# Kv and q loads gated by a step, four buffers for partial sums at a switch of segments, and one kv split moved

## The chip, the cores and the metric

The kernel runs on one core of one Trainium2 chip. Its time is the device time of one execution in microseconds (us), the median of several. TensorE (PE) multiplies, VectorE (DVE) and ScalarE (ACT) do the elementwise work, GpSimd (POOL) a little of it, and SyncE (SP) issues the DMAs. Each engine works through its own list of instructions in order.

## The reference

```python
def _attn_ref(q, k, v, g_norm):                  # q, k, v: 8 x 8 x 576 x 64
    kv = np.einsum('bhsd,bhse->bhde', k, v)
    out = np.einsum('bhsd,bhde->bhse', q, kv)
    rms = np.sqrt(np.mean(out * out, axis=-1, keepdims=True) + 1e-06)
    return (out / rms * g_norm).astype(np.float32)

def _moe_ref(x, w_in, w_out):                    # x: 4608 x 512
    h = x @ w_in                                 # w_in: 512 x 2048
    g = h * np.cos(h)
    return (g @ w_out).astype(np.float32)        # w_out: 2048 x 512
```

The heads' outputs are laid side by side into x (4608 tokens of 512 values), so the second function works on the first one's result. All is float32.

## The kernel before

**Tiling.** The 4608 tokens are cut into nine chunks of 512 (`NCH`). A chunk needs sixteen steps j, one for each 128 of the 2048 hidden values, 144 steps in all. Every float32 product is made of three matmuls on a high and a low part (`ghi`, `glo`; `xhi`, `xlo`; both halves of a split weight). A step has two blocks of twelve matmuls of 128x512: stage 1 is `bank<-x,wi`, stage 2 is `acc<-wo,g`, one step or two later, into four accumulators `acc0` to `acc3` in PSUM, one for each 128 tokens. Between them ACT and DVE compute h·cos h: ACT writes `ki`, DVE subtracts twice into `r`, ACT takes sine and square in `r`, DVE multiplies, ACT casts to `ghi`, DVE subtracts to `glo`.

**Segments.** The chunks do not run one behind the other at the start. The weights arrive during the first steps, so `segments` runs chunk 0 for j = 0 to 4, chunk 1 for j = 0 to 6, chunk 0 for 5 to 15, chunk 1 for 7 to 15, then chunks 2 to 8 whole. At the first two switches (behind step 4 and step 11) the sums in the accumulators are incomplete: `out_part` copies each to SBUF and writes it to DRAM (`part0_0` and so on, line 802). At the third switch and the next it loads them back (line 783) and adds them on DVE to the new sums, before the result goes out (line 799).

**Buffers.** `out_part` takes its SBUF tile from pool `osb`, two buffers, name `ob`. Pool `at` has three buffers for name `s1`, which the preparation of x uses (squares, then x itself). `kvp` has two buffers for each of `kt`, `vt`, `ktt`, `vtt`. The raw weights lie in one slot of `wpool` each, and before a weight is loaded its slot is lent to the early inputs. The slot of `wo15` is lent longest: it holds `kv_front`, the kv products of the first two batches (in the order they appear as tile `wo15_135`). `kv_split_part` splits the four of them that chunk 2 needs too into `kv_hi` (ACT) and `kv_lo` (DVE); only then may `wo15` be loaded.

**What sets the order.** The class `Order` is a planner that runs before the program does. Every piece of work is a generator that asks for `wait` (events), `take` (a token for a buffer) and `run` (an engine with a length and a priority, mostly a due time `due(i)` of a step i). The planner starts the work that can start first and, among equals, the lowest priority. In this way it fixes the order on PE, ACT, DVE and POOL, and the instructions are pinned in it. For a DMA it fixes when the load is asked for in the program; the framework places it on SP's queue and adds the semaphores. An event of the planner is no wait in the program. `gates[i]` is the event that fires when step i's first matmuls are planned.

All pinned instructions carry the helper's line L198. The other lines that occur are SP's: L327 and L329 the kv loads, L350 q, L380 weights, L783, L799 and L802 those of `out_part`.

Of the kernel before, what the change touches and what calls it, by code (L numbers as in the profile page):

```python
# [9 lines left out]
F32 = mybir.dt.float32  # L10
# [9 lines left out]
P = 128  # L20
# [127 lines left out]
def tile_kernel(  # L148
# [11 lines left out]
    B, H, S, D = q.shape  # L160
    NT, DM = out.shape
# [7 lines left out]
    SI = S // P  # L169
# [3 lines left out]
    FRONT = 2  # L173
# [5 lines left out]
    kvp = ctx.enter_context(tc.tile_pool(name="kvp", bufs=2))  # L179
    at = ctx.enter_context(tc.tile_pool(name="at", bufs=3))  # L180
    small = ctx.enter_context(tc.tile_pool(name="small", bufs=4))
    ew = ctx.enter_context(tc.tile_pool(name="ew", bufs=3))
    osb = ctx.enter_context(tc.tile_pool(name="osb", bufs=2))
# [3 lines left out]
    sched = Order()  # L187
# [14 lines left out]
    def dve_us(f=CH, rate=1):  # L202

        return 0.15 + f / (960 * rate)

    def act_us(f=CH):
        return 0.18 + f / 1200
# [10 lines left out]
    def dve_only(f):  # L218
        return [("DVE", 0.15 + f / 960)]
# [28 lines left out]
    steps, begin, need = [], {}, {}  # L248
# [10 lines left out]
    def due(i):  # L259

        return 24.0 + STEP * i + 0.8 * min(i, 14)

    def chunk_parts(c):
        parts, t = [], c * CH
        while t < (c + 1) * CH:
            b = t // S
            e = min((c + 1) * CH, (b + 1) * S)
            parts.append((b, t - b * S, t - c * CH, e - t))
            t = e
        return parts  # L270

    def chunks_of(b):
        return [c for c in range(NCH) if any(x[0] == b for x in chunk_parts(c))]

    def events(*dims):
        keys = [()]
        for n in dims:
            keys = [x + (i,) for x in keys for i in range(n)]
        return {x: Event() for x in keys}

    kv_in, kv_used, kv_done = events(B, NP), events(B, NP), events(B, NP)
    q_in, q_used, x_done = events(NCH, NP), events(NCH, NP), events(NCH, NP)
# [5 lines left out]
    t_kv, t_q, t_qT, t_two = Tokens(2), Tokens(2), Tokens(1), Tokens(3)  # L288

    t_bank, t_psa = Tokens(8 - NTT), Tokens(2)  # L290
    t_s1 = Tokens(3)
    t_x, t_h, t_ki, t_r, t_g, t_osb = Tokens(6), Tokens(3), Tokens(1), Tokens(3), Tokens(3), Tokens(2)
# [4 lines left out]
    DMA_LAT = 2.0  # L297

    def load(us, prio, event, issue, wait=(), take=None):
        def part():  # L300
            if wait:
                yield "wait", wait
            if take:
                yield "take", take
            _, end = yield "run", [("DMA", us)], prio
            issue()
            for ev in event:
                sched.fire(ev, end + DMA_LAT)
        sched.spawn(part())
# [9 lines left out]
    def kv_loads(b, p):  # L319
        def issue():  # L320
            kt = kvp.tile([P, 2, SI, D], F32, name="kt")
            vt = kvp.tile([P, 2, SI, D], F32, name="vt")
            ktt = kvp.tile([ST, 2, D], F32, name="ktt")
            vtt = kvp.tile([ST, 2, D], F32, name="vtt")
            h = slice(2 * p, 2 * p + 2)
            for t, src in ((kt, k), (vt, v)):
                nc.sync.dma_start(out=t, in_=src[b, h, 0:SI * P, :].rearrange("h (p i) d -> p h i d", i=SI))  # L327
            for t, src in ((ktt, k), (vtt, v)):
                nc.sync.dma_start(out=t, in_=src[b, h, SI * P:S, :].rearrange("h p d -> p h d"))  # L329
            kv_tiles[b, p] = kt, vt, ktt, vtt  # L330
        return issue
# [11 lines left out]
    def q_loads(c, p):  # L343
        def issue():
            qb = at.tile([P, TB, 32], F32, name="qb")
            for b, s0, o0, n in chunk_parts(c):
                for j in range(2):
                    for f in range(2):
                        e = 2 * j + f
                        nc.sync.dma_start(  # L350
                            out=qb[32 * e:32 * e + 32, o0 // 32:(o0 + n) // 32, :],
                            in_=q[b, 2 * p + j, s0:s0 + n, 32 * f:32 * f + 32].rearrange("(tb t) d -> t tb d", t=32),
                        )
            q_tiles[c, p] = qb
        return issue
# [82 lines left out]
    def kv_split_part(b, p, prio):  # L438

        yield "wait", [kv_done[b, p]]  # L440
        yield "run", [("ACT", 0.29)], prio
        act.copy(out=kv_hi[:, b % 2, p, :], in_=kv_front[:, b, p, :])
        _, end = yield "run", dve_only(P), prio
        dve.tensor_tensor(
            out=kv_lo[:, b % 2, p, :], in0=kv_front[:, b, p, :], in1=kv_hi[:, b % 2, p, :].bitcast(F32),
            op=ALU.subtract)
        sched.fire(kv_split[b, p], end)
# [231 lines left out]
    gates = [Event() for _ in steps]  # L679

    def window(c):

        first = last_step[c - 2] + 1
        return first, begin[c] - first
# [83 lines left out]
    def rows(c, t):  # L768
        if c < FRONT:
            return out[c * CH:(c + 1) * CH, :].rearrange("(r a) f -> a r f", a=NTT)[t]  # L770
        return out[c * CH + t * P:c * CH + (t + 1) * P, :]
# [3 lines left out]
    def out_part(c, t, acc, complete, prio):  # L775

        spare = c == NCH - 1 and t == NTT - 1
        yield "take", t_kv if spare else t_osb
        before = partial.pop((c, t), None)
        if before is not None:  # L780
            _, end = yield "run", [("DMA", 0.75)], prio
            o = osb.tile([P, DM], F32, name="ob")
            nc.sync.dma_start(out=o, in_=before)  # L783
            come = Event()
            sched.fire(come, end + DMA_LAT)
            yield "wait", [come]
            _, end = yield "run", [("DVE", dve_us(DM))], prio
            dve.scalar_tensor_tensor(out=o, in0=acc, scalar=-2.0, in1=o, op0=ALU.mult, op1=ALU.add)
        else:
            _, end = yield "run", [("ACT", act_us(DM))], prio  # L790
            if spare:
                o = kvp.tile([P, 2, SI, D], F32, name="kt").rearrange("p h i d -> p (h i d)")
            else:
                o = osb.tile([P, DM], F32, name="ob")
            act.activation(out=o, in_=acc, func=AF.Copy, scale=-2.0)
        sched.give(t_acc[t], end)
        _, end = yield "run", [("DMA", 0.75)], prio
        if complete:
            nc.sync.dma_start(out=rows(c, t), in_=o)  # L799
        else:  # L800
            partial[c, t] = tc.dram_tile([P, DM], F32, name=f"part{c}_{t}_{sched.seq}")
            nc.sync.dma_start(out=partial[c, t], in_=o)  # L802
        if not spare:
            sched.give(t_osb, end + DMA_LAT)


    lent, slots = {}, sorted(need, key=lambda x: (need[x], x))[-10 * FRONT - 1:]
# [11 lines left out]
    for c in range(FRONT):  # L819
        for p in range(NP):  # L820
            t = due(begin[c]) - 32 + 3 * p if c else -100.0 + p
# [7 lines left out]
    for c in range(FRONT):  # L829
        for p in range(NP):  # L830
            t = due(begin[c]) - 24 + 1 * p if c else -10.0 + 0.5 * p
# [3 lines left out]
        load(1.5, due(need[key]) - 10, [w_in[key]], w_loads(key), wait=lent.get(key, ()))  # L835
        sched.spawn(w_part(key, due(need[key]) - 4.0))
    for b, p in kv_split:
        sched.spawn(kv_split_part(b, p, due(begin[b]) + p))

    def gated(i, part):  # L840
        yield "wait", [gates[i]]
        yield from part

    for b in range(FRONT, B):
        first, n = window(chunks_of(b)[0])
        for p in range(NP):
            i = first + p * (n - 4) // NP
            load(2.1, due(i) - 6.0, [kv_in[b, p]], kv_loads(b, p),
                 wait=[x_done[0, 2], x_done[0, 3]], take=t_kv)
            sched.spawn(gated(i, kv_part(b, p, due(i + 4))))  # L850
    for c in range(FRONT, NCH):
        first, n = window(c)
        for p in range(NP):
            i = first + 1 + p * (n - 4) // NP
            load(1.96 * len(chunk_parts(c)), due(i) - 6.0, [q_in[c, p]], q_loads(c, p), take=t_q)
            sched.spawn(gated(i, x_part(c, p, due(i + 4))))
    for i in range(len(steps)):
        sched.spawn(stage1_part(i))
# [32 lines left out]
```

## Time and profile before

| | |
|---|---|
| median of 3 runs | 894.17 us (893.02 to 894.75) |
| the profiled execution | 894.57 us |
| its span in the trace | 892.8 us |
| PE busy | 876.0 us, 98% |
| DVE, ACT, POOL busy | 597.7, 512.0, 102.2 us |
| mean granted TensorE clock | 0.993 of full speed |

The profile records each instruction with its engine, its place and the operands by the program's names, out<-in. A timeline lists them in time; where an engine was idle before an instruction, brackets say for how long and which engine or DMA released it. The window view sums up stretches, with the clock that PE was granted. The list of waits groups idle time by who waited for whom. The chain follows the work back from the last instruction. Times are in us from the start of the span.

### The profile page before, as it was taken

The numbers are of one execution on the slowest core, as the hardware profiler recorded it, in microseconds if no ns is written. First come the engines' busy times: TensorE is split into PE (matmuls) and PEld (weight loads), VectorE is DVE, ScalarE is ACT, GpSimd is POOL, SyncE is SP. The second block draws the span as 40 slices with busy tenths as digits, with TensorE's granted clock in tenths as the row PEclk, the third lists the DMA queues.
The fourth block names the chain that finished last, engine by engine and source line by source line (L and its number), as shares of the span: only waits on it lengthen the run. The fifth ranks groups of instructions, "written<-read, shape, count | busy, mean of one in ns | idle before, by whom it ended". The sixth has DMA issues, their size and how long they took to land.

```text
span 892.8 us, 12407 instructions
## 1 busy us (share of the span) xinstructions
PE 876.0 (98%) x4648; PEld 720.5 (81%) x4648; DVE 597.7 (67%) x996; ACT 512.0 (57%) x997; POOL 102.2 (11%) x49
## 2 busy tenths in 40 slices
PE   9996999999999999999999999999999999999997
PEld 8785888778888888888888888888888888888886
DVE  3886789787777667665766567765776577654553
ACT  4785888664655556545655465555554566455444
POOL 3210000012211101120111011110221012100000
PEclk9999899999999999999999999999999999999999
DMA  9997020153132113110311022202200010001001
GB/s 299 342 294 192 23 72 1 48 159 89 51 99 51 27 31 93 39 39 9 109 43 42 1 86 66 50 2 63 63 12 12 4 56 1 1 1 47 1 1 47
DMA packets 103564, 59.53 MB, mean 67 GB/s; under 512 B 70224, under 2 KB 92752, under 8 KB 103504
## 3 DMA queue, kind: packets, MB, share of 16 engines
q1 hardware_dynamic: 103504, 58.75, 22.9%
q8 instruction: 36, 0.59, 0.3%
q14 instruction: 24, 0.20, 0.1%
HBM read 47.19 MB, written 11.53 MB: 66 GB/s over the span
## 4 chain that ended last, share of the span: by engine, by line
PE 95%; DMA 2%; SPq 1%; ACT 1%; DVE 1%; issue 0%; ACTq 0%
PE bank L198 50%; PE acc L198 44%; DMA wi<-in_v_dram 1%; DMA part<-ob 1%; DMA wo<-in_v_dram 1%; SPq L380 0%; DVE r L198 0%; SPq L338 0%; ACT r L198 0%; DVE sg L198 0%; ACT m L198 0%; ACT ob L198 0%; SPq L366 0%; DVE wi L198 0%; ACT ki L198 0%
## 5 line engine op out<-in xcount | busy, mean ns | idle before, releaser
L198 PE MATMUL acc<-wo,ghi 128*128 128x512 f32 x1152 | 359.5, 393 | 7.6 <-ACT ob L198 7.6
L198 PE MATMUL bank<-xhi,wi 128*128 128x512 f32 x1088 | 339.1, 393 | 1.6 <-DVE r L198 0.7
L198 PEld LDWEIGHTS acc<-wo,ghi 128*128 128x128 f32 x1152 | 215.4, 189 | 52.8 <-ACT ob L198 8.0
L198 PEld LDWEIGHTS bank<-xhi,wi 128*128 128x128 f32 x1088 | 202.6, 188 | 45.0 <-DVE r L198 1.1
L198 ACT ACTIVATE r<-r 128x512 f32<-128x512 f32 x288 | 181.7, 631 | 89.8 <-DVE r L198 85.9
L198 PE MATMUL acc<-wo,glo 128*128 128x512 f32 x576 | 225.0, 391 | 0.0
L198 PE MATMUL bank<-xlo,wi 128*128 128x512 f32 x544 | 212.0, 390 | 0.0
L198 POOL TENSOR_TENSOR rinv<-ms,mhalf 128x16 f32<-128x16 f32 (+1 forms) x36 | 99.4, 2761 | 671.8 <-DVE ms L198 671.8
L198 DVE SCALAR_TENSOR_TENSOR r<-ki,bank 128x512 f32<-128x512 int32 x144 | 98.6, 685 | 101.4 <-ACT ki L198 101.2
L198 ACT ACTIVATE ki<-bank 128x512 int32<-128x512 f32 x144 | 85.7, 595 | 125.1 <-PE bank L198 123.2
L198 DVE SCALAR_TENSOR_TENSOR r<-r,bank 128x512 f32<-128x512 f32 x144 | 98.5, 684 | 82.3 <-ACT r L198 81.8
L198 PEld LDWEIGHTS acc<-wo,glo 128*128 128x128 f32 x576 | 108.7, 189 | 23.0
L198 DVE TENSOR_TENSOR glo<-r,ghi 128x512 fp32r<-128x512 f32 x144 | 98.3, 683 | 39.1 <-ACT ghi L198 37.5
L198 PEld LDWEIGHTS bank<-xlo,wi 128*128 128x128 f32 x544 | 102.3, 188 | 21.5
L198 ACT CAST ghi<-r 128x512 fp32r<-128x512 f32 x144 | 89.1, 619 | 52.0 <-DVE r L198 51.3
L198 DVE SCALAR_TENSOR_TENSOR r<-ki,r 128x512 f32<-128x512 int32 x144 | 98.9, 687 | 2.1
L198 ACT ACTIVATE s<-bank 128x512 f32<-128x512 f32 x32 | 19.2, 599 | 26.4 <-PE bank L198 26.3
L198 ACT ACTIVATE ob<-acc 128x512 f32<-128x512 f32 x35 | 20.2, 597 | 16.9 <-DMA part<-ob 9.3
L198 DVE STREAM_TRANSPOSE s<-rinv 128x512 f32<-128x512 f32 x28 | 19.8, 708 | 12.9 <-POOL rinv L198 12.9
L198 DVE STREAM_TRANSPOSE qT<-s 128x512 f32<-128x512 f32 x28 | 19.9, 711 | 12.1 <-ACT s L198 11.7
L198 ACT COPY swp<-part 32x16 f32<-32x16 f32 x112 | 22.6, 202 | 9.1 <-DVE part L198 7.2
L198 ACT CAST kv_hi<-bank 64x64 fp32r<-64x64 f32 x48 | 9.9, 206 | 30.2 <-PE bank L198 29.9
(94 smaller groups left out, 566.6 us busy)
## 6 DMA issues: line engine op xcount, KB each, us to landing
out_dram<-ob SPq DMA_DIRECT2D x35, 256.0 KB, 2.2
wi<-in_moe_w_in_dram SPq DMA_DIRECT2D x16, 512.0 KB, 9.9
wo<-in_moe_w_out_dram SPq DMA_DIRECT2D x16, 512.0 KB, 8.7
kt<-in_k_dram SPq DMA_DIRECT2D x24, 256.0 KB, 2.8
vt<-in_v_dram SPq DMA_DIRECT2D x24, 256.0 KB, 3.2
part<-ob SPq DMA_DIRECT2D x8, 256.0 KB, 2.3
ob<-part SPq DMA_DIRECT2D x8, 256.0 KB, 2.9
qb<-in_q_dram SPq DMA_DIRECT2D x32, 48.0 KB, 2.1
```

Of the source, the lines that this page charges most:

```text
L198: return lambda *a, **kw: tc.keep_in_program_order(f(*a, **kw))
```

## The change

It has three parts. In `out_part` the token is taken with a priority, and from `t_s1` (pool `at`, name `s1`) for odd tiles t when the sum is partial, stored or reloaded; even tiles and complete sums stay in `osb`. In the list of early splits the priority of `kv_split_part` goes from the due time of the chunk that it belongs to (step 5) to that of chunk 2 (step 32) less 30 us. And the loads of later kv and q wait, in the planner, for the gate of the step `LEAD` = 7 ahead of their own.

```diff
--- before.py
+++ after.py
@@ -775,11 +775,18 @@
     def out_part(c, t, acc, complete, prio):
 
         spare = c == NCH - 1 and t == NTT - 1
-        yield "take", t_kv if spare else t_osb
         before = partial.pop((c, t), None)
+
+        tokens = t_kv if spare else t_s1 if t % 2 and not (complete and before is None) else t_osb
+        yield "take", tokens, prio
+        if tokens is t_s1:
+            o = at.tile([P, DM], F32, name="s1")
+        elif tokens is t_osb:
+            o = osb.tile([P, DM], F32, name="ob")
+        else:
+            o = kvp.tile([P, 2, SI, D], F32, name="kt").rearrange("p h i d -> p (h i d)")
         if before is not None:
             _, end = yield "run", [("DMA", 0.75)], prio
-            o = osb.tile([P, DM], F32, name="ob")
             nc.sync.dma_start(out=o, in_=before)
             come = Event()
             sched.fire(come, end + DMA_LAT)
@@ -788,10 +795,6 @@
             dve.scalar_tensor_tensor(out=o, in0=acc, scalar=-2.0, in1=o, op0=ALU.mult, op1=ALU.add)
         else:
             _, end = yield "run", [("ACT", act_us(DM))], prio
-            if spare:
-                o = kvp.tile([P, 2, SI, D], F32, name="kt").rearrange("p h i d -> p (h i d)")
-            else:
-                o = osb.tile([P, DM], F32, name="ob")
             act.activation(out=o, in_=acc, func=AF.Copy, scale=-2.0)
         sched.give(t_acc[t], end)
         _, end = yield "run", [("DMA", 0.75)], prio
@@ -801,7 +804,7 @@
             partial[c, t] = tc.dram_tile([P, DM], F32, name=f"part{c}_{t}_{sched.seq}")
             nc.sync.dma_start(out=partial[c, t], in_=o)
         if not spare:
-            sched.give(t_osb, end + DMA_LAT)
+            sched.give(tokens, end + DMA_LAT)
 
 
     lent, slots = {}, sorted(need, key=lambda x: (need[x], x))[-10 * FRONT - 1:]
@@ -835,7 +838,10 @@
         load(1.5, due(need[key]) - 10, [w_in[key]], w_loads(key), wait=lent.get(key, ()))
         sched.spawn(w_part(key, due(need[key]) - 4.0))
     for b, p in kv_split:
-        sched.spawn(kv_split_part(b, p, due(begin[b]) + p))
+        sched.spawn(kv_split_part(b, p, due(begin[FRONT]) - 30 + p))
+
+
+    LEAD = 7
 
     def gated(i, part):
         yield "wait", [gates[i]]
@@ -846,13 +852,13 @@
         for p in range(NP):
             i = first + p * (n - 4) // NP
             load(2.1, due(i) - 6.0, [kv_in[b, p]], kv_loads(b, p),
-                 wait=[x_done[0, 2], x_done[0, 3]], take=t_kv)
+                 wait=[x_done[0, 2], x_done[0, 3], gates[max(i - LEAD, 0)]], take=t_kv)
             sched.spawn(gated(i, kv_part(b, p, due(i + 4))))
     for c in range(FRONT, NCH):
         first, n = window(c)
         for p in range(NP):
             i = first + 1 + p * (n - 4) // NP
-            load(1.96 * len(chunk_parts(c)), due(i) - 6.0, [q_in[c, p]], q_loads(c, p), take=t_q)
+            load(1.96 * len(chunk_parts(c)), due(i) - 6.0, [q_in[c, p]], q_loads(c, p), wait=[gates[max(i - LEAD, 0)]], take=t_q)
             sched.spawn(gated(i, x_part(c, p, due(i + 4))))
     for i in range(len(steps)):
         sched.spawn(stage1_part(i))
```

PE, ACT and POOL run the same instructions in number. Three places of the order show what moved. A name is a tile with its running number; `[waits ...]` are the semaphores that the instruction waits for, DMAHW being DMAs.

ACT at the first switch, where `ob` (and after, `s1`) receives an accumulator; before:

```order
L198 CAST wi5_1040<-sg_950 128x512 [waits DVE_49]
L198 ACTIVATE ob_1047<-acc0_681 128x512 [waits PE_49]
L198 ACTIVATE ob_1053<-acc1_693 128x512 [waits PE_49]
L198 CAST ghi_1059<-r_984 128x512 [waits DVE_49]
L198 ACTIVATE r_1042<-r_1042 128x512 [waits DVE_49]
L198 ACTIVATE sg_1078<-wo6_678 128x512 [waits DMAHW2_49,DVE_49]
L198 ACTIVATE r_1042<-r_1042 128x512 [waits Activation_49]
L198 ACTIVATE ki_1100<-bank2_1009 128x512 [waits PE_49]
L198 CAST wi6_1107<-sg_964 128x512 [waits DVE_49]
L198 ACTIVATE ob_1114<-acc2_703 128x512 [waits DMAHW1_49]
L198 ACTIVATE ob_1117<-acc3_708 128x512 [waits DMAHW2_49]
```

After:

```order
L198 CAST wi5_1030<-sg_940 128x512 [waits DVE_49]
L198 CAST wi6_1038<-sg_962 128x512 [waits DVE_49]
L198 ACTIVATE ob_1037<-acc0_681 128x512 [waits PE_49]
L198 CAST ghi_1051<-r_996 128x512 [waits DVE_49]
L198 ACTIVATE s1_1044<-acc1_693 128x512 [waits PE_49]
L198 ACTIVATE ob_1050<-acc2_703 128x512 [waits PE_49]
L198 ACTIVATE s1_1062<-acc3_708 128x512 [waits PE_49]
L198 ACTIVATE r_1032<-r_1032 128x512 [waits DVE_49]
L198 ACTIVATE ki_1087<-bank2_1007 128x512 [waits Activation_49]
L198 ACTIVATE r_1032<-r_1032 128x512 [waits Activation_49]
```

The four copies now stand close together with a cast of `ghi` among them, in four different buffers, and wait for PE alone; before, the last two waited for DMAs.

DVE where the fourth early split, `kv_lo_86<-wo15_135`, stands; before, among the operations of chunk 0's step 4 and chunk 1's first:

```order
L198 TENSOR_TENSOR glo_942<-r_877,ghi_941 128x512 [waits Activation_49]
L198 SCALAR_TENSOR_TENSOR r_948<-ki_932,r_948 128x512 [waits DVE_49]
L198 SCALAR_TENSOR_TENSOR sg_884<-wo4_614,sg_884 128x512 [waits DMAHW6_49]
L198 TENSOR_TENSOR kv_lo_86<-wo15_135,kv_hi_85 128x128
L198 SCALAR_TENSOR_TENSOR sg_950<-sg_950,m_958 128x512 [waits Activation_49]
L198 SCALAR_TENSOR_TENSOR r_984<-ki_977,bank1_918 128x512 [waits Activation_49]
```

After, among those of chunk 1's last weights (`wo14`, `wo15`), 133 rows further down:

```order
L198 SCALAR_TENSOR_TENSOR r_1811<-ki_1801,r_1811 128x512 [waits DVE_49]
L198 SCALAR_TENSOR_TENSOR sg_1742<-wo14_987,sg_1742 128x512 [waits DMAHW6_49,DVE_49]
L198 TENSOR_TENSOR kv_lo_86<-wo15_135,kv_hi_85 128x128
L198 TENSOR_TENSOR wo14_1849<-sg_1742,wo14_1849 128x512 [waits Activation_49]
L198 SCALAR_TENSOR_TENSOR r_1811<-r_1811,bank1_1745 128x512 [waits Activation_49]
L198 TENSOR_TENSOR glo_1866<-r_1811,ghi_1865 128x512 [waits PE_49,Activation_49]
L198 SCALAR_TENSOR_TENSOR r_1886<-ki_1872,bank3_1820 128x512 [waits Activation_49]
L198 SCALAR_TENSOR_TENSOR r_1886<-ki_1872,r_1886 128x512 [waits DVE_49]
L198 TENSOR_SCALAR m_1915<-wo15_1860 128x512 [waits DMAHW2_49]
L198 TENSOR_TENSOR kv_lo_86<-bank0_1888,kv_hi_85 64x64 [waits Activation_49]
L198 TENSOR_TENSOR kv_lo_86<-bank0_1888,kv_hi_85 64x64
L198 SCALAR_TENSOR_TENSOR sg_1913<-sg_1913,m_1915 128x512 [waits DVE_49,Activation_49]
```

The split moved, and the conversion of `wo15` (m_1915, sg_1913) follows it six rows later, waiting for its DMA.

SP, the DMAs of the switches, from the load of `wi15` on; before:

```order
L380 DMA wi15_971<-in_moe_w_in_dram 128x4x128
L380 DMA wo15_1003<-in_moe_w_out_dram 128x512
L802 DMA part0_0_924_1068<-ob_1047 128x512
L802 DMA part0_1_932_1076<-ob_1053 128x512
L802 DMA part0_2_967_1137<-ob_1114 128x512
L802 DMA part0_3_973_1145<-ob_1117 128x512
L802 DMA part1_0_1181_1421<-ob_1413 128x512
L802 DMA part1_1_1186_1429<-ob_1418 128x512
L802 DMA part1_2_1214_1463<-ob_1452 128x512
L802 DMA part1_3_1219_1472<-ob_1461 128x512
L783 DMA ob_2041<-part0_0_924_1068 128x512
L783 DMA ob_2058<-part0_1_932_1076 128x512
```

After:

```order
L380 DMA wi15_971<-in_moe_w_in_dram 128x4x128
L805 DMA part0_0_895_1056<-ob_1037 128x512
L805 DMA part0_1_907_1070<-s1_1044 128x512
L805 DMA part0_2_911_1077<-ob_1050 128x512
L805 DMA part0_3_915_1085<-s1_1062 128x512
L805 DMA part1_0_1162_1411<-ob_1384 128x512
L805 DMA part1_1_1168_1422<-s1_1391 128x512
L805 DMA part1_2_1172_1430<-ob_1402 128x512
L790 DMA ob_1973<-part0_0_895_1056 128x512
L805 DMA part1_3_1178_1441<-s1_1408 128x512
L790 DMA ob_1997<-part0_2_911_1077 128x512
L380 DMA wo15_1860<-in_moe_w_out_dram 128x512
L327 DMA kt_1837<-in_k_dram 128x2x256
```

The load of `wo15` went from the place ahead of all partial writes to one behind them and behind two reloads; the first kt load comes next in both (`kt_1868` before).

SP at the third switch, where partial sums of chunk 0 are loaded back; before:

```order
L327 DMA kt_2070<-in_k_dram 128x2x256
L327 DMA vt_2071<-in_v_dram 128x2x256
L329 DMA ktt_2072<-in_k_dram 64x2x64
L329 DMA vtt_2073<-in_v_dram 64x2x64
L799 DMA out_0_dram<-ob_2041 128x512
L799 DMA out_0_dram<-ob_2058 128x512
L350 DMA qb_2217<-in_q_dram 32x6x32 x2
L783 DMA ob_2174<-part0_2_967_1137 128x512
L350 DMA qb_2217<-in_q_dram 32x6x32
L783 DMA ob_2182<-part0_3_973_1145 128x512
```

After:

```order
L327 DMA kt_1976<-in_k_dram 128x2x256
L327 DMA vt_1977<-in_v_dram 128x2x256
L329 DMA ktt_1978<-in_k_dram 64x2x64
L329 DMA vtt_1979<-in_v_dram 64x2x64
L350 DMA qb_2091<-in_q_dram 32x4x32 x3
L790 DMA s1_1988<-part0_1_907_1070 128x512
L790 DMA s1_2003<-part0_3_915_1085 128x512
L350 DMA qb_2091<-in_q_dram 32x4x32
L350 DMA qb_2091<-in_q_dram 32x12x32 x4
```

The reloads of tiles 1 and 3 now go to `s1` and stand ahead of the outputs of chunk 0, behind one kv load and three q loads; before, the reloads of tiles 2 and 3 stood behind the outputs of the first two.

## Rows read from the trace of the kernel before

**Rows 1.** The page, busy time of each engine and share of the span
```profile
PE 876.0 (98%) x4648; PEld 720.5 (81%) x4648; DVE 597.7 (67%) x996; ACT 512.0 (57%) x997; POOL 102.2 (11%) x49
```

**Rows 2.** Windows: stretch, length; busy (x) of PE PEld DVE ACT POOL; PEclk, DMA, GB/s
```profile
81.70:89.30 7.60, 0.03 (x2) 0.01 (x1) 0.00 (x0) 0.64 (x2) 0.00 (x0) 0.72 0.60 198
89.30:95.30 6.00, 6.00 (x14) 4.76 (x15) 4.62 (x8) 6.00 (x12) 0.00 (x0) 0.50 0.23 87
180.00:200.00 20.00, 19.29 (x133) 15.06 (x132) 17.05 (x31) 12.64 (x29) 2.90 (x1) 1.00 0.58 156
```

**Rows 3.** Waits, whole run: engine, what it waited for, total us, times, longest
```profile
ACT ob L198 <- DMA part<-ob: 9.3, 1, 9.3
...
PE acc L198 <- ACT ob L198: 7.6, 1, 7.6
```

**Rows 4.** Timeline of PE at the first switch: start, length, work, [idle before]
```profile
81.33 0.39 PE L198 MATMUL bank<-xlo,wi 128*128 128x512 f32 x1
89.29 0.80 PE L198 MATMUL acc<-wo,ghi 128*128 128x512 f32 x1 [7.57 <-ACT ob L198]
...
95.59 0.63 PE L198 MATMUL acc<-wo,ghi 128*128 128x512 f32 x2
```

**Rows 5.** Chain of the last work, 74 to 96: start, length, what
```profile
74.24 2.73 PE acc L198 x12
...
80.62 8.00 DMA part<-ob
```

**Rows 6.** Timeline of ACT at the first switch
```profile
74.96 1.28 ACT L198 ACTIVATE ob<-acc 128x512 f32<-128x512 f32 x2 [1.10 <-PE acc L198]
...
88.64 1.22 ACT L198 ACTIVATE ob<-acc 128x512 f32<-128x512 f32 x2 [9.27 <-DMA part<-ob]
```

**Rows 7.** Timeline of SP, DMA issues, the same stretch
```profile
80.16 0.37 SPq L380 DMA_DIRECT2D wo<-in_moe_w_out_dram  x1
80.62 0.86 SPq L802 DMA_DIRECT2D part<-ob  x2
```

**Rows 8.** Timeline of DVE, 65 to 69
```profile
65.14 0.68 DVE L198 TENSOR_TENSOR xlo<-s,xhi 128x512 fp32r<-128x512 f32 x1
...
68.15 0.28 DVE L198 TENSOR_TENSOR kv_lo<-wo,kv_hi 128x128 fp32r<-128x128 f32 x1
```

**Rows 9.** Timeline of DVE, 170 to 175
```profile
170.53 0.68 DVE L198 SCALAR_TENSOR_TENSOR r<-r,bank 128x512 f32<-128x512 f32 x1
...
174.57 0.69 DVE L198 SCALAR_TENSOR_TENSOR r<-ki,r 128x512 f32<-128x512 int32 x1
```

**Rows 10.** Landing (us) of a wo load of 512 KB at 65.5:67, and of tile wo
```profile
wo<-in_moe_w_out_dram SPq DMA_DIRECT2D x1, 512.0 KB, 5.3
...
DMA to landing us min/median/max: 3.1/7.9/11.3
```

**Rows 11.** The page, DMA issues: count, KB each, median us to landing
```profile
vt<-in_v_dram SPq DMA_DIRECT2D x24, 256.0 KB, 3.2
...
ob<-part SPq DMA_DIRECT2D x8, 256.0 KB, 2.9
```

**Rows 12.** Timeline of PE, 177 to 182
```profile
177.19 0.69 PE L198 MATMUL bank<-vt,kt 128*64 128x64 f32 x16
...
181.89 0.50 PE L198 MATMUL acc<-wo,ghi 128*128 128x512 f32 x1
```

**Rows 13.** Timeline of DVE and SP around the third switch
```profile
189.68 1.28 DVE L198 SCALAR_TENSOR_TENSOR ob<-acc,ob 128x512 f32<-128x512 f32 x2
...
200.17 1.25 DVE L198 SCALAR_TENSOR_TENSOR ob<-acc,ob 128x512 f32<-128x512 f32 x2
...
184.30 2.60 SPq L350 DMA_DIRECT2D qb<-in_q_dram  x5
```

**Rows 14.** Timeline of SP and of PE, one later load and its use
```profile
346.34 0.46 SPq L327 DMA_DIRECT2D vt<-in_v_dram  x1
...
381.48 0.69 PE L198 MATMUL bank<-vt,kt 128*64 128x64 f32 x16
```

## The prediction

> **What bounds the kernel now.** I read first the busy time of each engine: PE works 876.0 of a span of 892.8 us, DVE 597.7 and ACT 512.0 [rows 1]. So 16.8 us at most can be won while PE's work stays as it is, and it does: the diff touches no product. The next view is the waits over the whole run, read for one large single wait of PE. There is one: PE waits 7.6 us, once, for an `ob` that ACT writes, and ACT itself waits 9.3 us, once, for a DMA that reads `ob` [rows 3]. The timelines of PE, ACT and SP and the chain of work then place it at the first switch of segments, behind step 4.
>
> There ACT copies accumulators 0 and 1 out at 74.96 and accumulators 2 and 3 only at 88.64, 9.27 us of that waiting [rows 6]. The pool `osb` has two buffers, so the third copy needs the first one's write to DRAM to be over. That write is issued at 80.62, behind a last weight load at 80.16 [rows 7], and takes 8.00 us in the chain [rows 5]. PE starts its last matmul before the stall at 81.33 and its next at 89.29 [rows 4].
>
> The price is more than the idle time. Twelve matmuls take 2.73 us at the full clock [rows 5], 0.2275 each, so PE was free at 81.33 + 0.23 = 81.56, and idle for 7.73 us. After it the granted clock is 0.50, that is the lower of the two levels, 1.2 GHz instead of 2.4: 14 matmuls fill 6.00 us [rows 2]. One more begins before 95.59, from which a matmul has its old length again [rows 4]. These 15 take 95.59 − 89.29 = 6.30 us instead of 15 × 0.2275 = 3.41, a loss of 2.89. The first switch costs 7.73 + 2.89 = 10.62 us, most of what PE has to lose.
>
> **The change part by part.** *Four buffers at a switch.* `out_part` now takes odd tiles of a partial sum from pool `at` (name `s1`), even ones from `osb`. The order of ACT shows the four copies with a wait for PE only, where two waited for a DMA. A buffer of `s1` must be free for that: chunk 1's x is finished with it at 65.14 [rows 8], and the order has no other user of the pool until chunk 2 is prepared. So the whole wait goes, unless another takes its place. What is late next? The four accumulators fill 0.68 us apart (three matmuls), so the last is full 2.05 us after the first. ACT needs five operations of 0.64 us (1.28 for two [rows 6]), the four copies and one `ghi`: the last copy ends about 3.2 us after the first accumulator was full. PE then has six stage-1 matmuls (1.37 us) ahead of the first accumulator's next use, at 2.05 + 1.37 = 3.4 us, and asks for the last at 5.5. ACT is ahead by 2 us. The copies themselves, four on ACT, are the same number as before, and the writes are the same eight DMAs. A DVE idle time and ACT's 9.27 us go with PE's. With no idle there is no reason in the rows for the lower clock behind it. Term: **−10.62**; the other end is 0, if the wait stays.
>
> *An early kv is split later.* Three of four splits keep their place; the fourth moves on DVE from 68.15 [rows 8] to a place just ahead of an operation that stood at 170.53 [rows 9]. It adds no instruction: 0.28 us of DVE and one ACT cast leave one place and come in at another, where PE does not wait for them. What counts is its DMA. The split's source lies in the slot of `wo15`, so `wo15`'s load waits for it. Before, that load went out at 80.16 [rows 7], 100 us ahead of PE's use at 181.89 [rows 12]; now it goes out at about 170.6. It is 512 KB; the same transfer landed in 5.3 us when little else ran, and the tile's landings lie between 3.1 and 11.3 with a median of 7.9 [rows 10]. I take 5.3, since SP has no other load in flight at that place but the reload of a partial sum: landing at 175.9. DVE asks for it in the row behind the operation at 174.57 [rows 9], at 175.2, and would wait 0.7 us. From landing to a split `wo15` there are five dependent operations of about 0.69, 3.5 us: 179.4, against 181.89. PE doesn't see it: 0.
>
> So the old place hides any landing, and the new one hides it up to about 7 us. The Trainium skill, "DMA: Bandwidth & Descriptors", section "Rules for kernel authors", says to issue a DMA early and to wait on its semaphore late, so that its fixed cost overlaps with compute. That rule speaks against this edit: where it decides, the time is the first rival's, 884.4 to 887.8, and where the 5.3 us of the row does, the sum below.
>
> *What is queued behind `wo15` on SP*: the kt and vt loads of the first gated batch. `wo15`, kt and vt are issued about 0.4 us apart (0.37 [rows 7]), vt at 171.4; with the page's landing of 3.2 [rows 11] it is there at 174.6. Its matmuls stood at 177.19 [rows 12]; in the new order of PE they stand ahead of one block of twelve more, at 177.19 − 2.73 = 174.46. So PE waits 0.1 us; if the two loads share the queue with `wo15` and land with it at 175.9, 1.4 us. No gain is possible, since PE has work there anyway. I take **+0.4**, nearer to the page's landing.
>
> *Third switch*, where partial sums are reloaded and added. Before, the adds ran in two pairs, at 189.68 and 200.17, the second pair behind the write of the first [rows 13]; now all four stand in a row on DVE. PE is idle for 20.00 − 19.29 = 0.71 us there [rows 2], which is the most that can be won. Against it: the two reloads into `s1` stand on SP at the place that five q loads held from 184.30 to 186.90 [rows 13]. With the median landing of 2.9 [rows 11] they are there between 187.2 and 190.2, about when the second add (189.68 + 0.64) wants one; with 5.3 [rows 10] at 192.5, 2.2 us late. Term −0.7 to +2.2, taken as **0**, by the page's landing. At the second switch PE does not wait in either order; 0.
>
> *Loads wait for a step near their use (`LEAD`).* These are events of the planner; in the program they add no wait. The order of SP has the loads where they were, and they already waited for a buffer. 0.
>
> **Sum**: the profiled execution took 894.57 us. 894.57 − 10.62 + 0.4 = 884.35. It lies 0.40 above the median of 894.17, so against the median **884.0 us**.
>
> **Rivals.** *First: `wo15` comes late.* At a landing of 7.9 it is there at 178.5; the conversion ends at 182.0, 0.1 behind PE, but DVE has meanwhile held back the `r` of the next step: five operations of 0.69, a cast and a subtraction end at 182.7, 0.8 us late. At 11.3 it is 4.2. On 883.6, the sum without its 0.4, that gives 884.4 to 887.8, and up to 888 with the kv loads behind it. For it: the median of the tile. Against: those landings come from a time when loads stood in line, and 5.3 was measured in a quiet stretch.
>
> *Second: DVE waits at the third switch* for a reload, in order, with four adds in a row and other work behind. Price 0.7 to 2.2 us: 884.7 to 886.2, up to 887 with the lower clock for a few matmuls. For it: the place of the reloads behind loads that wait for PE. Against: the page's landing just fits.
>
> *Third: the gate holds the later loads back until they are late.* Price: 24 vt loads of 3.2 us [rows 11], 77 us, and a time near 961. Against it: a load's issue at 346.34 is used at 381.48 [rows 14], 35 us later, in an order of SP that doesn't change; only the first groups have less.
>
> *Fourth: the change doesn't do what it says*: the copies still wait, because an `s1` buffer isn't free or the write of the first `ob` holds a place in front; then 894.2 stays. Against it stand 65.14 [rows 8] and the waits in the order of ACT.
>
> *Fifth, slower than before*: `wo15`'s load, in the first rival's place, so late that its loss beats the gain. To pass 894.17 + 1.8 it must cost 12.4 us; with 2.89 of lower clock behind an idle of that length, 9.5 us idle, a landing 17 us after the issue. It decides from there; the longest in the rows is 11.3. Time: 896 to 899.
>
> **How the numbers follow.** About 0.2%, 1.8 us, is what a measurement of this kernel can tell from no change. Chances: forecast 0.64, with 882.8 to 885.2 as its own range (0.7 won at the third switch and 0.4 unspent below, 1.2 above); `wo15` late 0.18; third switch 0.08; loads late 0.02; no effect 0.04; `wo15` so late that it is slower 0.04. Faster by over 0.2% is 0.64 + 0.18 + 0.08 = 0.90, no change 0.04, slower 0.04 + 0.02 = 0.06. The range runs from 882.0 (a little of PE's other idle time after 160 is won too) to 888.0, the end of the first rival, and holds about 0.88 of it before the misreadings that I can't name.
>
> **What would show it.** The waits lose the 7.6 us of PE behind `ob` and the 9.3 of ACT; the window 80 to 100 has PE busy throughout at a clock of 1.00; partial writes leave from four buffers. For the second part: the load of `wo15` between 155 and 165 (all is 10.6 earlier), and whether DVE waits for it, and PE for DVE, near 171. For the third: DVE's wait ahead of the adds near 179. Wrong it would be if PE shows a new single wait of some us behind a weight, a kv or an accumulator, or if PE begins to wait for DVE in the stretch behind the first switch, whose pause gave DVE and ACT time too.

## The result: 882.83 us, and the profile after

The changed kernel takes 882.83 us, median of 4 runs (882.62 to 883.86), beside 894.46 (893.02 to 895.16) for the kernel before. The ratio is 0.9874, 95% interval 0.9857 to 0.9891, so 11.3 us less (9.7 to 12.8). Forecast were 884.0, range 882.0 to 888.0. The profiled execution took 882.62 us with a span of 880.8; PE is busy for 873.6 us of it, 99%.

The windows of after that answer to [rows 2] (length; busy time and count of PE, PEld, DVE, ACT, POOL; granted clock, DMA share, GB/s):

```profile
80.00:100.00 20.00, 20.00 (x90) 16.57 (x89) 18.11 (x31) 16.64 (x31) 0.00 (x0) 1.00 0.26 90
160.00:180.00 20.00, 20.00 (x138) 15.91 (x137) 14.26 (x29) 11.19 (x26) 0.36 (x1) 1.00 0.64 175
180.00:200.00 20.00, 20.00 (x108) 16.50 (x107) 17.89 (x31) 11.64 (x25) 4.95 (x2) 1.00 0.64 168
```

PE is busy throughout, at full clock, where before it stood still for 7.57 us and then ran at half the clock, and also from 180 to 200, where 0.71 us were idle before. (PE's work now runs some 10.6 us earlier, so these windows do not hold the same work as before; but PE has no idle time anywhere from 80 to 230.) The list of waits has no wait of PE for `ob` and none of ACT for a DMA of partial sums; both rows of [rows 3] are gone.

ACT and SP at the first switch, which answer to [rows 6] and [rows 7] (start, length, work, idle before):

```profile
76.23 0.60 ACT L198 ACTIVATE ob<-acc 128x512 f32<-128x512 f32 x1 [1.10 <-PE acc L198]
76.72 0.61 ACT L198 CAST ghi<-r 128x512 fp32r<-128x512 f32 x1
77.23 0.60 ACT L198 ACTIVATE s<-acc 128x512 f32<-128x512 f32 x1
77.72 0.60 ACT L198 ACTIVATE ob<-acc 128x512 f32<-128x512 f32 x1
78.27 0.60 ACT L198 ACTIVATE s<-acc 128x512 f32<-128x512 f32 x1
```

```profile
77.14 0.45 SPq L805 DMA_DIRECT2D part<-ob  x1
77.86 0.38 SPq L805 DMA_DIRECT2D part<-s  x1
78.35 0.39 SPq L805 DMA_DIRECT2D part<-ob  x1
78.90 0.36 SPq L805 DMA_DIRECT2D part<-s  x1
```

All four copies leave within 2.6 us, one after the other as PE fills the accumulators. Each partial write starts within 0.4 us of the end of its copy. The writes are about as slow as before: these four landed 7.6 us after their issue at the median (last column, us), where the first one took 8.00 before. But nobody waits for them.

```profile
part<-ob SPq DMA_DIRECT2D x2, 256.0 KB, 7.6
part<-s SPq DMA_DIRECT2D x2, 256.0 KB, 7.6
```

The moved load and the work around it, which answer to [rows 8, 9, 12]: SP, DVE, PE, and the landing of the three loads (us, last column).

```profile
158.43 0.33 SPq L380 DMA_DIRECT2D wo<-in_moe_w_out_dram  x1
158.96 0.38 SPq L327 DMA_DIRECT2D kt<-in_k_dram  x1
159.39 0.46 SPq L327 DMA_DIRECT2D vt<-in_v_dram  x1
```

```profile
158.08 0.28 DVE L198 TENSOR_TENSOR kv_lo<-wo,kv_hi 128x128 fp32r<-128x128 f32 x1
...
164.55 0.42 DVE L198 TENSOR_SCALAR m<-wo 128x512 int32<-128x512 uint32 x1
```

```profile
163.84 0.69 PE L198 MATMUL bank<-vt,kt 128*64 128x64 f32 x16
...
171.26 0.50 PE L198 MATMUL acc<-wo,ghi 128*128 128x512 f32 x1
```

```profile
wo<-in_moe_w_out_dram SPq DMA_DIRECT2D x1, 512.0 KB, 3.3
kt<-in_k_dram SPq DMA_DIRECT2D x1, 256.0 KB, 3.9
vt<-in_v_dram SPq DMA_DIRECT2D x1, 256.0 KB, 4.1
```

`wo15` is asked for at 158.43, right behind the end of the split, and is there at 161.7. DVE begins its conversion at 164.55 with no idle time in front: it came to that row later than the data. (One `m<-wo` has gone from ACT to DVE: ACT has 996 instructions and DVE 997, where they had 997 and 996, so ACT's number is not quite the same as before.) The vt load behind it landed at 159.39 + 4.1 = 163.5, and PE uses it at 163.84.

The third switch, which answers to [rows 13]: DVE's four adds, and the reloads into `s1`.

```profile
180.69 0.69 DVE L198 SCALAR_TENSOR_TENSOR ob<-acc,ob 128x512 f32<-128x512 f32 x1
181.30 0.68 DVE L198 SCALAR_TENSOR_TENSOR s<-acc,s 128x512 f32<-128x512 f32 x1
181.89 0.68 DVE L198 SCALAR_TENSOR_TENSOR ob<-acc,ob 128x512 f32<-128x512 f32 x1
182.49 0.68 DVE L198 SCALAR_TENSOR_TENSOR s<-acc,s 128x512 f32<-128x512 f32 x1
```

```profile
174.93 0.90 SPq L790 DMA_DIRECT2D s<-part  x2
...
s<-part SPq DMA_DIRECT2D x2, 256.0 KB, 3.0
```

The reloads landed 3.0 us behind their issue, at 178.4 at the latest (the second issue begins inside the row's 0.90 us), over 2 us ahead of the second add.

### The profile page after: what moved, and what is told of

The parts are those of the page before. It is cut to its first block, busy times and chain, and to the rows that moved or that the text cites. A ratio compares the mean times of both kernels' runs of the same rounds, so it can differ in the third digit from the quotient of the medians.

```text
span 880.8 us, 12406 instructions
## 1 busy us (share of the span) xinstructions
PE 873.6 (99%) x4648; PEld 719.4 (82%) x4648; DVE 598.2 (68%) x997; ACT 510.9 (58%) x996; POOL 102.7 (12%) x49
## 4 chain that ended last, share of the span: by engine, by line
PE 98%; DMA 0%; ACT 0%; DVE 0%; issue 0%; SPq 0%; ACTq 0%
PE bank L198 53%; PE acc L198 46%; DMA wo<-in_v_dram 0%; DVE sg L198 0%; DVE r L198 0%; ACT s L198 0%; ACT ob L198 0%; ACT kt L198 0%; ACT m L198 0%; ACT r L198 0%; SPq L338 0%; ACTq L198 0%
## 5 line engine op out<-in xcount | busy, mean ns | idle before, releaser
L198 DVE STREAM_TRANSPOSE s<-rinv 128x512 f32<-128x512 f32 x28 | 19.8, 706 | 10.6 <-POOL rinv L198 10.6
L198 ACT CAST xhi<-s 128x512 fp32r<-128x512 f32 x32 | 19.6, 618 | 6.4 <-DVE s L198 5.4
```

What stands on the lines that cost most here:

```text
L198: return lambda *a, **kw: tc.keep_in_program_order(f(*a, **kw))
```

## The experiments

Times of the kernels are medians, and ratios are to runs of the kernel before on the same chip, with their 95% interval.

| kernel | us | ratio | interval |
|---|---|---|---|
| four buffers alone | 882.65 | 0.9879 | 0.9864 to 0.9893 |
| later split alone | 891.99 | 0.9982 | 0.9959 to 1.0005 |
| gate alone | 894.12 | 1.0007 | 0.9995 to 1.0019 |
| buffers and split | 882.82 | 0.9883 | 0.9869 to 0.9898 |
| buffers and gate | 882.80 | 0.9883 | 0.9865 to 0.9901 |
| split and gate | 892.34 | 0.9994 | 0.9983 to 1.0006 |
| three buffers | 891.71 | 0.9993 | 0.9981 to 1.0004 |
| stall filled with matmuls of zeros | 891.50 | 0.9984 | 0.9974 to 0.9994 |
| ACT issues the partial writes | 886.69 | 0.9933 | 0.9912 to 0.9954 |
| whole change, split held to step 23 | 883.76 | 0.9896 | 0.9881 to 0.9911 |
| whole change, split held to step 24 | 886.72 | 0.9923 | 0.9907 to 0.9940 |
| whole change, LEAD 0 | 887.01 | 0.9932 | 0.9915 to 0.9949 |

**Which part pays.** The three parts were taken one at a time and in pairs. Theory: the two buffers make the stall. Rival: the weight loads ahead of the partial writes on SP make it.

Four buffers alone (the diff of `out_part` only, nothing else changed):

> The four buffers alone; the split and the loads are as before. Theory (two buffers make the stall): PE's 7.6 us wait and the lower clock behind it go, 10.6 us, and the time is 883 to 885, within 1.5 us of the whole change. Rival (the stall is made by the weight loads that stand ahead of the partial writes on SP, so the moved split is needed too): PE still waits some us at the first switch, 888 to 893.

Later split alone:

```diff
-        sched.spawn(kv_split_part(b, p, due(begin[b]) + p))
+        sched.spawn(kv_split_part(b, p, due(begin[FRONT]) - 30 + p))
```

> The later split alone, two buffers. The load of wo15 no longer stands ahead of the first partial writes. Theory: the third copy still waits for the first write; that write starts about 0.5 us sooner and has 512 KB less ahead of it, some 1.7 us at the 300 GB/s of the page's busiest slices, so the stall is 5 to 6 us plus 2.9 of lower clock: 891 to 893. Rival (the queue is the cause): stall under 2 us, 883 to 886.

Gate alone (`LEAD` = 7 in both loads):

> The gate on later loads alone. It adds no wait to the program, but frees the planner's model of the DMA queue and so moves some work of PE and ACT around the first switch. Theory: the stall stays, 892.5 to 895.5. Rival (the gate makes loads late): above 896, with PE waiting for kt or vt. Rival (the gate is what pays): below 888.

The pairs:

> Four buffers and the later split, without the gate. Theory: as the whole change, 882 to 884.5. If the gate matters (for or against) it is off by over 2 us from 882.8.

> Four buffers and the gate, split as before. After the run with four buffers alone at 882.65: 882 to 884. If the later split is worth something beside the buffers, over 884.5.

> Later split and gate, two buffers: a stall at the first switch remains, 889 to 894. If two buffers are enough once both other parts are in: 883 to 885.

With four buffers all of these kernels lie at 882.7 to 882.8, whatever else is in them, and without at 892 to 894. (Single executions of the later split alone scatter most, from 887.31 to 897.24 us.) The four buffers are the whole gain; the later split and the gate add nothing that these runs could tell from zero, with the buffers or without. The windows of four buffers alone are those of the whole change:

```profile
80.00:100.00 20.00, 20.00 (x90) 16.56 (x89) 18.20 (x31) 16.51 (x31) 0.00 (x0) 1.00 0.37 132
180.00:200.00 20.00, 20.00 (x109) 16.52 (x108) 17.18 (x30) 11.51 (x25) 4.98 (x2) 1.00 0.56 143
```

The four buffers alone also refute the rival: the load of `wo15` still stands ahead of the partial writes on SP there, and the first write is issued even later than the 80.62 of the kernel before, yet PE doesn't wait.

```profile
78.58 2.98 SPq L380 DMA_DIRECT2D wo<-in_moe_w_out_dram  x1
81.65 0.38 SPq L805 DMA_DIRECT2D part<-ob  x1
```

The later split alone shows the same from the other side. The chain of work at its first switch, and PE:

```profile
78.83 7.52 DMA part<-ob
```

```profile
87.08 1.22 PE L198 MATMUL acc<-wo,ghi 128*128 128x512 f32 x2 [3.22 <-ACT ob L198]
...
250.14 1.22 PE L198 MATMUL acc<-wo,ghi 128*128 128x512 f32 x2 [2.27 <-DVE ob L198]
```

With no `wo15` ahead of it, the partial write starts at 78.83 instead of 80.62, yet takes 7.52 us where it took 8.00. So PE still waits 3.22 us for `ob` (less than the 5 to 6 expected: in its order PE has work until 83.70 instead of 81.56), and a new wait of 2.27 us came at 250.14, at the next switch, behind an add for which DVE waited 1.9 us, until a reload had landed. That is the mechanism of the prediction's second rival, one switch later and in a kernel with two buffers.

**How many buffers.** Tile 1 alone goes to `s1`, tile 3 waits for the first write as before:

```diff
-        tokens = t_kv if spare else t_s1 if t % 2 and not (complete and before is None) else t_osb
+        tokens = t_kv if spare else t_s1 if t == 1 and not (complete and before is None) else t_osb
```

> Four buffers less one: only tile 1 of a partial sum goes to the other pool, tile 3 waits for the first write as before; nothing else is changed. Theory (PE needs the accumulators in a row, so the last copy's wait is a wait of the same end): PE goes on three matmuls (0.7 us) further and then waits to the same instant, with the lower clock behind: 891 to 894. Rival (every buffer is worth its share): 887 to 889.

Two lines of the list of waits (total us, times, longest):

```profile
ACT ob L198 <- DMA part<-ob: 7.7, 1, 7.7
PE acc L198 <- ACT ob L198: 6.0, 1, 6.0
```

891.71 us, ratio 0.9993: three buffers are worth nothing that the times can tell from zero (0.6 us less, between 1.7 less and 0.4 more), as the theory had it. This kernel also has the new priority of `take`, so that isn't the gain either. The longest wait in the list is 7.7 us of ACT and 6.0 of PE instead of 9.3 and 7.6. The fourth copy still waits for the same write, and PE needs it a moment later.

**What the stall is made of.** Two runs on the kernel before take its 10.6 us apart. The first keeps PE at work while it waits:

```diff
+                if i == 5 and t == 2:
+                    for _ in range(110):
+                        pe.matmul(out=accs[0][:, 0:P], lhsT=zeros, rhs=zeros, start=False, stop=False)
```

> The kernel before, with 110 small matmuls of zeros put on PE where it stalls at the first switch (they add zero to accumulator 0). The wait for the copy stays. Theory (the lower clock behind the stall comes from PE standing idle and costs 2.9 us of the 10.6): the clock behind the wait is 1.00, and the time falls by 2 to 3 us, to 890.2 to 891.5. Rival (the lower clock has another cause): no change, 892.5 to 894.5, clock 0.50 behind the wait.

PE's timeline and a window behind the wait:

```profile
81.96 6.32 PE L198 MATMUL acc<-zeros 128*128 128x128 bf16 x110
88.91 0.73 PE L198 MATMUL acc<-wo,ghi 128*128 128x512 f32 x2 [0.64 <-ACT ob L198]
```

```profile
88.91:95.00 6.09, 6.09 (x27) 5.03 (x28) 4.71 (x8) 6.09 (x12) 0.00 (x0) 1.00 0.24 89
```

The wait ends at 88.91 as before (89.29), and behind it the clock is 1.00: 27 matmuls in 6.09 us, where before 14 filled 6.00. So the lower clock came from PE standing idle. By the trace that is worth the 2.89 us of the sum; the times say 0.9984 (0.9974 to 0.9994), 1.4 us (0.5 to 2.3), less than the 2 to 3 expected. The clocks of other executions suggest why: the one on which the 2.89 was read is one of the dearer ones. Its mean granted clock is 0.993. Of the 53 executions of the kernel before that were timed beside the runs, 13 have that clock and take 894.3 us on average; the 22 with 0.996 take 892.7. So the order of sizes is right, and 2.89 is the price in one execution, not the usual one.

The second moves the partial writes off SP's line:

```diff
-            nc.sync.dma_start(out=partial[c, t], in_=o)
+            tc.keep_in_program_order(nc.scalar.dma_start(out=partial[c, t], in_=o))
```

> The kernel before with two buffers, but ACT issues the partial writes instead of SP, where eight q loads and four weight loads stand ahead of them. Theory (the write's own transfer is slow because the engines are busy): it is issued some 5 us sooner and still takes about 8, so the stall is near 3 us plus 2.9 of lower clock: 887 to 890. Rival (place in SP's line is all of it): it lands in 2 to 4 us, no stall, 882.5 to 885.

The first two writes on ACT's queue, ACT's third and fourth copies, and PE:

```profile
77.75 0.38 ACTq L802 DMA_DIRECT2D part<-ob  x1
78.39 0.33 ACTq L802 DMA_DIRECT2D part<-ob  x1
...
81.94 0.60 ACT L198 ACTIVATE ob<-acc 128x512 f32<-128x512 f32 x1 [1.00 <-DMA part<-ob]
85.16 0.60 ACT L198 ACTIVATE ob<-acc 128x512 f32<-128x512 f32 x1 [2.62 <-DMA part<-ob]
```

```profile
82.59 0.74 PE L198 MATMUL acc<-wo,ghi 128*128 128x512 f32 x2 [0.48 <-ACT ob L198]
85.81 0.72 PE L198 MATMUL acc<-wo,ghi 128*128 128x512 f32 x2 [2.25 <-ACT ob L198]
```

886.69 us, ratio 0.9933. The writes start at 77.75 and 78.39, some 2.9 us sooner and not 5, since the first waited for a q load to end. They landed after 4.2 and 6.75 us, and the third and fourth copies follow them at 81.94 and 85.16. PE waits 0.48 and 2.25 us, and in this execution the clock stays at 1.00 behind that. So the place in SP's line is a part of the stall, and the slow transfer another; neither rival was right alone. Both are out of the way once nobody waits for the write.

**The cover of the moved load.** The whole change, with the fourth split held back in the planner (the second run has `gates[24]`):

```diff
-        yield "wait", [kv_done[b, p]]
+        yield "wait", [kv_done[b, p]] + ([gates[23]] if p == NP - 1 else [])
```

> The whole change, and the moved split held back further, to the first matmuls of step 23 (the load of wo15 goes out behind four kv loads). Prices the first rival of the prediction. In the profile of the change the load was issued at 158.43, landed in 3.3 us, and its conversion could wait until about 167.8 for PE's use at 171.26, so some 6 us are to spare. About 4 us are taken here: 882.3 to 884 if the cover holds; over 884.5 if the landing grows or the conversion is held up.

> As the run before, held back to step 24: the load is issued near 168 to 170 and the conversion ends near 177 to 179, past 171.26, while the planner puts two stage-1 blocks (5.4 us) ahead. Theory (the cover was about 6 us and is gone): PE waits 0.5 to 3 us for wo15, the lower clock may follow: 883.5 to 888. Rival (stage-1 work always hides it): 882.3 to 883.5.

At step 23 it costs nothing clear: 883.76, ratio 0.9896 with an interval that overlaps that of the change (0.9857 to 0.9891). Yet the cover as it was worked out was used up. The load was issued at 164.23, landed in 5.7 us, and DVE waited for it:

```profile
169.96 0.43 DVE L198 TENSOR_SCALAR m<-wo 128x512 int32<-128x512 uint32 x1 [1.18 <-DMA wo<-in_moe_w_out_dram]
```

The conversion thus began 2.2 us behind the 167.8 of the expectation. PE didn't wait, because the order that the planner made for this kernel has eighteen stage-1 matmuls ahead of the next use of a `wo`, which comes at 175.57. At step 24 it costs some 4 us, 886.72 beside 882.83. PE, SP and DVE there, and a window behind PE's wait:

```profile
179.37 1.22 PE L198 MATMUL bank<-xhi,wi 128*128 128x512 f32 x2 [1.81 <-DVE r L198]
```

```profile
170.90 0.38 SPq L380 DMA_DIRECT2D wo<-in_moe_w_out_dram  x1
```

```profile
178.30 0.41 DVE L198 TENSOR_SCALAR m<-wo 128x512 int32<-128x512 uint32 x1
178.63 0.68 DVE L198 SCALAR_TENSOR_TENSOR r<-r,bank 128x512 f32<-128x512 f32 x1
```

```profile
179.40:182.00 2.60, 2.60 (x6) 2.14 (x7) 2.60 (x5) 1.99 (x4) 0.00 (x0) 0.50 0.88 256
```

The load is issued at 170.90, 12.5 us later than in the change. Yet the wait is not for its landing: DVE comes to the conversion at 178.30 without idle time. PE has run stage-1 blocks ahead and waits 1.81 us, for an `r` that frees a bank of PSUM. As I read DVE's timeline, it had its normal work, the conversion and the preparation of chunk 2 to do at once. Then the clock is 0.50 for the six matmuls of the window. The price foreseen (0.5 to 3 us and the clock) came about, by another way than foreseen.

**A gate that is too near.**

```diff
-    LEAD = 7
+    LEAD = 0
```

> The whole change with LEAD 0 instead of 7, so the loads of later kv and q come into the program at the step near their use. Rival three of the prediction (loads late) has its best chance here. Theory (the gate puts no wait into the program and the loads wait for their buffers anyway): 882 to 884. Rival: PE waits for kt, vt or a q load in several groups, 0.5 to 3 us each: over 886.

PE's waits for DVE in that kernel, from the list of waits (total us, times, longest); behind the first 20 us it has none for a load of k, v or q:

```profile
PE bank L198 <- DVE r L198: 2.4, 2, 2.0
PE bank L198 <- DVE s L198: 1.0, 1, 1.0
```

887.01 us, some 4 more than with LEAD 7. The time is in the range of the rival, but its mechanism isn't there: behind the first 20 us, whose waits for early v loads the kernel before has too, no engine waits for a load of kv or q. PE waits 2.0 us once for an `r` and 1.0 for an `s` of DVE, both from 180 to 230, where the preparation of chunks 2 and 3 now crowds. That it is the crowding I read from the order of DVE; no run tested it by itself.

## Why the prediction was right, step by step

**The stall.** The term of −10.62 us is confirmed in mechanism and about in size. PE is busy from 80 to 100, and the buffers alone bring all of the gain: 0.9879 of 893.24, so 10.8 us less (9.6 to 12.1), the 0.95 us below included. Both halves of it were read rightly: the idle time goes when no copy waits for a write (three buffers against four), and the lower clock behind it comes from the idle time (the filled stall), though 2.89 us is its price in the execution that was profiled.

**ACT ahead by 2 us.** It was: the last copy ends at 78.87, PE asks for that accumulator at 81.47, and doesn't wait for it. The four copies run at 76.23 to 78.87 with `ghi` among them, as worked out.

**`wo15`.** Issue near 160, landing in 5.3 us, a wait of 0.7 us of DVE and none of PE: it was 158.43, 3.3 us, and no wait of either. The bound that mattered was not the landing at all; DVE came to the conversion 2.8 us after it.

**kt and vt behind it.** The +0.4 us is not there. vt landed in 4.1 us, slower than the 3.2 that I took, but it was issued 12.0 us earlier than the 171.4 of the working and used 10.6 us earlier (163.84 for 174.46), so it was in time by 0.3 us. The mis-sized step is the issue time: I put the split right ahead of the operation that stood at 170.53, and it began 1.4 us ahead of it (158.08 and 159.45).

**The third switch.** Taken as 0, it won: 0.71 us of idle time from 180 to 200 are gone, and 0.24 from 160 to 180 (a wait for a `wi` of DVE), where my sum didn't look. The window of the kernel before there:

```profile
160.00:180.00 20.00, 19.76 (x102) 15.79 (x101) 15.18 (x27) 12.42 (x24) 0.00 (x0) 1.00 0.20 66
```

The lower end of the bounds was the right one. The reloads were issued at 174.93, 1.2 us behind the 184.30 − 10.6 of the working, and landed over 2 us before they were wanted.

**The sum.** With the terms as the traces show them, 894.17 − 10.62 − 0.71 − 0.24 = 882.6, and 882.83 was measured. That it closes so well is in part luck: 894.17 is the median of three executions, and that of the 53 later ones is 893.16, from which the same terms give 881.6. The forecast of 884.0 was 1.2 us too high, by the +0.4 for kt and vt that wasn't there and by the third switch and the 0.24, for which it had nothing; 882.83 is at the lower edge of the 882.8 to 885.2 that it took for its own.

**The rivals.** `wo15` late: not here, and holding the split back cost nothing clear until step 24, where the price was DVE's crowding and not the landing. The rival assumed that the order around `wo15` stays; held back further, the planner put other work ahead. DVE waiting for a reload: not here, but it is in the profile of the later split alone. The gate: it adds no wait to the program, but it isn't the nothing that I costed. At LEAD 0 some 4 us are lost without a wait for these loads, as I read it by the planner's order. With LEAD 7 it comes out at zero, which I had right for a reason that is too simple.

## What to carry to other kernels

When a copy out of PSUM waits for the write of an earlier one, count the accumulators that PE needs in a row: buffers for all of them take the stall away, one more than before only shortens it, and here that bought nothing that the times could show. Price such a stall with the matmuls behind it at the lower clock, not with the idle time alone, and read that price in more than one execution. And where a planner sets the order, a wait that exists only in the plan still moves pinned work, so its price is read from the order and not from the program's waits.

## What the runs showed of the hardware

The length of an idle time did not tell what the lower clock behind it would cost. The table has the five profiles in which PE stood idle at the first switch and then ran at a granted clock of 0.50, the lower of its two levels (1.2 and 2.4 GHz): the matmuls of 512 columns from the end of the wait until one has its old length, the time they took, and what that is above 0.2275 us each.

| kernel | idle, us | matmuls | time, us | lost, us |
|---|---|---|---|---|
| before | 7.57 | 15 | 6.30 | 2.89 |
| gate alone | 7.83 | 12 | 5.13 | 2.40 |
| three buffers | 5.99 | 12 | 5.25 | 2.52 |
| split and gate | 5.26 | 8 | 3.33 | 1.51 |
| later split alone | 3.22 | 14 | 6.08 | 2.90 |

The least idle time has as dear a stretch behind it as nearly the greatest. Two windows of the later split alone, behind its 3.22 us and behind the 2.27 us at the next switch:

```profile
87.30:92.30 5.00, 5.00 (x12) 3.91 (x13) 3.62 (x7) 5.00 (x11) 0.00 (x0) 0.50 0.27 105
250.20:253.00 2.80, 2.80 (x7) 2.22 (x8) 2.75 (x7) 1.16 (x2) 0.00 (x0) 0.50 0.62 221
```

Behind 1.81 us, with the split held to step 24, six matmuls ran at 0.50; behind 2.25 us, where ACT issues the writes, none did:

```profile
86.00:92.00 6.00, 6.00 (x27) 4.94 (x27) 5.42 (x9) 6.00 (x12) 0.00 (x0) 1.00 0.27 103
```

What else decides it these runs don't say.

A write of 256 KB took 2.3 us at the median of the kernel before's eight, but the first one, behind the weight loads, between 7.3 and 8.0 us in the five profiles with two buffers in which SP issues it, and still 4.2 and 6.75 us when another queue issued the first two while those loads ran. An earlier place in line alone did not make it fast.
